# Second pair's scores as single float32 products, under a re-searched table and dearer planner charges

## The chip, the cores and the metric

One core of one Trainium2 chip runs the whole program in one launch. The metric is device time in microseconds. The kernel before took 822.62 us (median of 3 runs, 822.43 to 823.08).

## The reference

The program computes an attention layer and two feed-forward layers on its output, all in float32.

```python
B, H, S, D = 4, 8, 576, 64
scores = scale * q @ k^T                      # per batch and head, 576 x 576
scores = where(block_i >= block_j, scores, -1e9)   # blocks of 64 positions
attn = exp(scores - max) / (sum + 1e-9);  x = attn @ v   # -> 2304 x 512
h = x @ w_in (512 x 2048); g = s * relu(h)**2 + b;  x = g @ w_out
h = max(x @ w1, x @ w2, x @ w3) (512 x 768);  out = h @ w_out2
```

## The kernel before, in words

Attention goes by pairs of heads: 16 pairs (4 batches, 4 pairs each). Columns of the two heads of a pair stand side by side in one tile. For each head there are four score units of 128 queries, 192, 320, 448 and 576 keys wide (`unit`, the last in two products of 288), and one unit for the first 64 queries of both heads (`first`, products of 64 by 64). A unit's maximum is taken by VectorE (`most`), its exponential by ScalarE (`expo`). The exponentials are transposed on TensorE (`turned`, 25 transposes a pair, L628), copied from PSUM, and multiplied with the values (`product`), one pair late.

Scores are made in one of two ways. In pairs 1 to 15 each operand is split into a float32r high part and a low part (`prep_pair`: khi, qhi, klo, q2, qlo), and each unit has two float32r products: one of 128 rows (`K1`, `Q1`) and one of 68 rows (`KQ`, whose last four rows carry the mask). Pair 0 alone is made otherwise (`prep_first`): its loaded rows are float32 operands as they are, 64 rows of data and the mask's rows below, in `xf`, a buffer that is not in use yet, and each unit is one plain float32 product.

The two heads' value products, and the two heads' `first` products, use TensorE as two arrays side by side (64 columns each). Both are gathered in a list and issued together by `side_by_side` wherever the order string has a `|`. This text calls such a run a visit. Value products read 128 rows; `first` reads 64 rows. The results leave PSUM by `put` (into `xf`), from bank 7, which the next pair's first value product needs again.

Behind attention come the feed-forward layers: three passes with plain tiles of 512 tokens (`l1`, `l2`), then tiles of 768 tokens by a seven-product scheme (`seven`) with float32r products of 384 columns (`l2_half`, `l4`). Weights are prepared on the way (`prepare_direct`, `prepare_aside`) and fetched again from a scratch in memory (`next_b`).

Nothing is issued in the order in which it is written. `op` records every operation with its possible engines, a cost on each, its dependencies, and a rank: its number plus the offset of its kind from `CFG['off']`. `Sched.run` then lets each engine take, at each point of the planned time, the ready operation of the lowest rank, and the program is issued in that order; on the chip each engine keeps to it and waits where its operand is late. The order of the steps of a pair is a string: a digit is a score unit, lower-case letters a to e turn exponentials, A to E multiply with values, p prepares the next pair, v loads values, `|` issues the visit. `order0` and `order1` are for pairs 0 and 1, `order` for the others. At the start 60 small products on zeros (`warm`, L1135 makes the zeros) have the highest rank of all: the planner puts one wherever TensorE has nothing else, until the 60 are used up. They are called fillers here. They are instructions in TensorE's queue and take their time, whatever the rest does.

Of the kernel before, what the change touches and what calls it, by code (L numbers as in the profile page):

```python
# [24 lines left out]
C0 = 192  # L25
NU = 4
# [3 lines left out]
EPS = 1e-9  # L30

# [57 lines left out]
def c_pooltt(n):  # L89
    return 2.4 * n + 100  # L90
# [64 lines left out]
class Sched:  # L155
# [45 lines left out]
    def run(self):  # L201
# [26 lines left out]
        while len(order) < n:  # L228
# [54 lines left out]
def tile_attention_moe(ctx: ExitStack, tc: tile.TileContext, qk, vp, w_in, w_out, ms_, b_, w123, w_out2, out):  # L283
# [98 lines left out]
    def load(size, f, eng="SP", after=(), lat=2000, **k):  # L382

        k["after"] = [op(eng, 380, f, lat=lat, after=after, **k)]
        return op("DMA", size / (CFG["rate"] if k.get("kind") in ("w", "w2", "wf") else 330), lambda e: None, lat=1000 + CFG["dm"].get(k.get("kind"), 0), **k)
# [37 lines left out]
    def load_pair(p):  # L423

        b, hp = divmod(p, H // 2)
        R = FIRST[0::2] if p == 0 else [rings["raw"].get() for _ in range(2)]
        if p == 0:

            for i, e_ in enumerate(("SP", "ACT")):
                def f(e, i=i):  # L430
                    (nc.sync if i == 0 else nc.scalar).dma_start(out=R[i].ap[0:64, 0:2 * S], in_=qk[b, hp, 0:64, i])
                load(294912, f, e_, lat=1260, writes=[(R[i], k) for k in ALL])
        else:
            for i in range(2):
                def f(e, i=i):
                    nc.sync.dma_start(out=R[i].ap, in_=qk[b, hp, :, i])
                load(589824, f, lat=2000 if p < 3 else CFG["dlat"], writes=[(R[i], k) for k in ALL])
        return R

    def prep_first():  # L440

        K0, (K, Q, R) = rings["k0"].get(), FIRST
        for x, keys, _, n in parts(0):
            q, q2 = qcols(R.ap, x, 0)[0:64], qcols(Q.ap[:, 0:1024], x, 64)[0:64]
# [3 lines left out]
            op(pick("q2", 0, **hi_cost(n)), 0, f, reads=[(R, k) for k in keys], writes=[(Q, k) for k in keys], kind="prep", lock=True)  # L448
            if x == "a":
                def f(e):  # L450
                    mul_to(e, K0.ap[:, 0:128], K.ap[0:64, 512:640], SCALE)
                op(pick("k0", 0, **hi_cost(128)), 0, f, reads=[(K, k) for k in keys], writes=[(K0, 0)], kind="prep0", lock=True)

                def f(e, q=q):
                    mul_to(e, K0.ap[:, 128:256].rearrange("p (h c) -> p h c", h=2), R.ap[0:64].rearrange("p (h c) -> p h c", h=2)[:, :, 0:64], 1.0)
                op(pick("k0", 0, **hi_cost(128)), 0, f, reads=[(R, k) for k in keys], writes=[(K0, 1)], kind="prep0", lock=True)
        return K0, None, None, None

    def prep_pair(p, R):


        if p == 0:
            return prep_first()
# [49 lines left out]
    def load_values(p):  # L513
# [5 lines left out]
        load(557056, f, lat=2000 if p < 2 else CFG["dlat"], writes=[V])  # L519
        return V  # L520

    def softmax_pair(p, P, DEN):
# [8 lines left out]
        def most(u, m, reads, v, n, axis=AX.X):  # L531
            def f(e):
                nc.vector.tensor_reduce(out=NM.ap[:, u:u + m], in_=v, axis=axis, op=ALU.max, negate=True)  # L533
            op("DVE", c_dve(n), f, reads=reads, writes=[(NM, u + i) for i in range(m)], kind="max")
# [21 lines left out]
        def scores(i, h, views, SB):  # L556
            keys = [(h, x) for x in ("a" if i == 0 else "ab")]
            K, Q, _ = FIRST

            def f(e):  # L560
                for o, c in views:
                    if p == 0:
                        mm(o, Q.ap[:, 512 * h + 128 * i:512 * h + 128 * i + 128], K.ap[:, c], True, True)
# [4 lines left out]
            op("PE", sum(2 * c_mm(c.stop - c.start) if p else c_two(4 * (c.stop - c.start)) for _, c in views), f,  # L568
                    reads=[(t, k) for k in keys for t in (K1, Q1)] + [(Q1, ("l",) + k) for k in keys] + [(KQ, (x,) + k) for k in keys for x in range(2)]
                    if p else [(t, k) for k in keys for t in (K, Q)] + [(K, "m"), (Q, "m")],  # L570
# [38 lines left out]
    def values_pair(p, E, V):  # L609
# [7 lines left out]
        def turn(groups, u):  # L617
# [3 lines left out]
            for g in groups:  # L621
# [11 lines left out]
                op({x: y(n) for x, y in (("ACT", c_act), ("DVE", c_dve)) if x in CFG["pe"]}, 0, f,  # L633
# [12 lines left out]
        def put(O, src, tok):  # L646
            n = src.stop - src.start

            def f(e):
                copy_to(e, xf[:, hp, t0 + tok:t0 + tok + n], O.ap[:, src])  # L650
            after_side.append(lambda: op({x: y(n) for x, y in (("ACT", c_act), ("DVE", c_dve)) if x in CFG["je"]}, 0, f, reads=[O],
                                         writes=[(XF, (hp, b, tok))], after=[i for u in FIRST for i in u.ops] if b > 1 else (), kind="jc"))
# [491 lines left out]
    flat = xf[:].rearrange("p k t -> p (k t)")  # L1144

# [285 lines left out]
    with tc.manual_schedule():  # L1431
# [5 lines left out]
CFG = {'aside': (6, 9, 12, 14, 18, 19, 23),  # L1437
        'aside3': (1, 1, 1, 0, 0, 0, 2, 0, 0, 2, 2, 0, 1, 1, 0, 2),
# [118 lines left out]
```

## Time and profile before

| | |
|---|---|
| median of 3 runs | 822.62 us |
| the profiled execution, its own time | 822.2 us |
| its span, first to last instruction | 820.4 us |
| busy: TensorE, its weight loads, VectorE, ScalarE, GpSimd | 814.6, 741.4, 616.7, 479.3, 64.6 us |
| TensorE's granted clock | full speed |

The profiled execution took 1.8 us more than its span, and 0.4 us less than the median. The span has two large parts: attention up to about 159 us, and the feed-forward layers behind it. In the timeline a row joins like instructions that follow each other: start, time to the modelled end of the last one, engine, line, operation, tiles, form of the first, count. Ends overlap with the next row, so the time that a group takes of TensorE is the start of the next row less its own start. A plain float32 product shows as two records, a float32r product and a transpose as one; the two heads' products of a visit are two instructions with two records each.

### The profile page before, as it was taken

Reading aid. Unit: us, or ns where it says so; the run is one execution under the profiler, and the core shown is the slowest. Engines: PE = TensorE matmul, PEld = TensorE weight load, DVE = VectorE, ACT = ScalarE, POOL = GpSimd, SP = SyncE. Lnnn points to the kernel's source line nnn. Section 1 sums busy time; section 2 is a strip of 40 time slices with the busy share of each in tenths; the row PEclk is TensorE's granted clock in tenths of the full one; section 3 lists DMA queues with packets and bytes.
Section 4 is the critical chain, followed back from the end, with each engine's and each line's share of the span. In section 5 each row is a group of like instructions: output and inputs, shape, how many; then the busy total and the mean of one; then the engine's idle time right before and its main releaser. Section 6 shows DMA issues by size and latency. Waiting matters only on the chain. (4 is left out here: it accounts for less than half of the span.)

```text
span 820.4 us, 14499 instructions
## 1 busy us (share of the span) xinstructions
PE 814.6 (99%) x4898; PEld 741.4 (90%) x4898; DVE 616.7 (75%) x1347; ACT 479.3 (58%) x1100; POOL 64.6 (8%) x57
## 2 busy tenths in 40 slices
PE   9999999999999999999999999999999999999998
PEld 7778887878888899999999999999999899999996
DVE  7889999998778898879967997986557245833551
ACT  6888989986665688689666669622143122412111
POOL 5344254000000000000000000000000000000000
PEclk9999999999999999999999999999999999999999
DMA  7877786465678599899679799899676477666742
GB/s 236 256 253 210 230 275 208 177 192 198 228 262 305 211 302 354 307 353 376 203 271 323 259 319 338 291 306 306 212 232 206 142 228 229 181 194 188 225 128 77
DMA packets 92178, 200.77 MB, mean 245 GB/s; under 512 B 10948, under 2 KB 16452, under 8 KB 92100
## 3 DMA queue, kind: packets, MB, share of 16 engines
q1 hardware_dynamic: 91880, 199.41, 73.2%
q8 instruction: 39, 0.64, 0.3%
q10 hardware_dynamic: 224, 0.43, 0.2%
q14 instruction: 35, 0.29, 0.1%
HBM read 152.24 MB, written 43.85 MB: 239 GB/s over the span
## 5 line engine op out<-in xcount | busy, mean ns | idle before, releaser
L380 PE MATMUL ps<-arena 128*128 128x384 f32 (+4 forms) x3834 | 719.7, 347 | 1.4 <-DVE arena L1135 1.2
L380 PEld LDWEIGHTS ps<-arena 128*128 128x128 f32 x3834 | 668.9, 188 | 43.3 <-issue 1.4
L959 ACT ACTIVATE other<-ps 128x384 f32<-128x384 f32 x154 | 75.0, 487 | 186.8 <-PE ps L380 169.3
L954 DVE TENSOR_TENSOR other<-ps,other 128x384 f32<-128x384 f32 x129 | 71.2, 554 | 106.2 <-PE ps L380 90.0
L377 DVE TENSOR_TENSOR arena<-other,arena 128x384 fp32r<-128x384 f32 (+3 forms) x201 | 117.9, 598 | 5.2 <-ACT arena L364 2.3
L538 ACT ACTIVATE other<-ps,other 128x192 f32<-128x192 f32 (+4 forms) x144 | 77.7, 550 | 14.9 <-DVE other L533 14.5
L366 DVE TENSOR_SCALAR arena<-other 128x384 fp32r<-128x384 f32 (+3 forms) x148 | 60.2, 410 | 29.6 <-PE ps L380 19.7
L372 ACT ACTIVATE other<-ps 128x512 f32<-128x512 f32 (+1 forms) x102 | 55.8, 572 | 40.3 <-PE ps L380 36.2
L533 DVE TENSOR_REDUCE other<-ps 128x1 f32<-128x192 f32 (+4 forms) x144 | 66.9, 513 | 8.1 <-PE ps L380 7.3
L628 PEld LDWEIGHTS ps<-ident,other 128*128 128x128 f32 x400 | 43.9, 141 | 15.4 <-ACT other L538 10.7
L380 PE MATMUL ps<-other 128*64 128x64 f32 (+5 forms) x640 | 55.1, 313 | 0.0
L377 DVE TENSOR_TENSOR other<-other 128x256 fp32r<-128x256 f32 (+1 forms) x125 | 52.7, 433 | 1.6 <-ACT other L364 0.6
L760 ACT ACTIVATE other<-other 128x512 f32<-128x512 f32 x64 | 43.1, 676 | 17.8 <-DVE other L756 17.8
L628 PE MATMUL ps<-ident,other 128*128 128x128 f32 x400 | 53.4, 277 | 0.0
L768 DVE SCALAR_TENSOR_TENSOR other<-other 128x512 uint32<-128x512 uint32 x64 | 43.6, 687 | 6.7 <-ACT other L760 6.2
L364 ACT ACTIVATE other<-other 128x256 fp32r<-128x256 f32 (+2 forms) x95 | 39.0, 426 | 12.2 <-DMA bscr<-other 4.9
L1345 ACT ACTIVATE other<-other,cst 128x384 f32<-128x384 f32 x64 | 44.7, 701 | 0.7
L364 ACT ACTIVATE arena<-other 128x384 fp32r<-128x384 f32 (+1 forms) x66 | 36.4, 562 | 13.2 <-DVE other L377 10.2
L380 PEld LDWEIGHTS ps<-other 128*64 128x64 f32 (+1 forms) x640 | 26.9, 136 | 13.8 <-issue 9.7
L374 DVE COPY other<-ps 128x384 f32<-128x384 f32 (+2 forms) x49 | 28.2, 597 | 14.2 <-ACT other L372 11.9
L377 POOL TENSOR_TENSOR arena<-other,arena 64x1152 fp32r<-64x1152 f32 x11 | 37.8, 3436 | 11.9 <-PE ps L380 7.4
L1330 ACT ACTIVATE other<-other 128x384 f32<-128x384 f32 x48 | 24.8, 520 | 17.3 <-DVE other L954 17.2
(46 smaller groups left out, 426.7 us busy)
## 6 DMA issues: line engine op xcount, KB each, us to landing
arena<-bscr SPq DMA_DIRECT2D x301, 256.0 KB, 3.3
bscr<-other SPq DMA_DIRECT2D x119, 256.0 KB, 4.0
other<-qk SPq DMA_DIRECT2D x30, 576.0 KB, 5.1
other<-w_in SPq DMA_DIRECT2D x24, 512.0 KB, 5.0
other<-w_out SPq DMA_DIRECT2D x22, 512.0 KB, 5.4
other<-w SPq DMA_DIRECT2D x18, 512.0 KB, 6.1
other<-vp SPq DMA_DIRECT2D x16, 544.0 KB, 5.0
other<-pscr SPq DMA_DIRECT2D x24, 192.0 KB, 4.3
```

The source lines that it names most:

```text
L364: nc.scalar.activation(out=dst, in_=src, func=AF.Copy, scale=m)
L366: nc.vector.tensor_scalar(out=dst, in0=src, scalar1=m, scalar2=None, op0=ALU.mult)
L372: nc.scalar.activation(out=dst, in_=src, func=AF.Copy)
L377: eng[e].tensor_tensor(out=dst, in0=a, in1=b, op=ALU.subtract)
L380: nc.tensor.matmul(o, l, r, start=start, stop=stop, **k)
L533: nc.vector.tensor_reduce(out=NM.ap[:, u:u + m], in_=v, axis=axis, op=ALU.max, negate=True)
L538: nc.scalar.activation(out=ev, in_=v, func=AF.Exp, bias=NM.ap[:, u:u + 1], scale=1.0, accum_out=DEN.ap[:, d:d + 1])
L628: nc.tensor.transpose(TB.ap[:, 128 * i:128 * i + 128], x, ident)
L768: nc.vector.scalar_tensor_tensor(out=lo_w, in0=hi_w, scalar=3, in1=lo_w, op0=ALU.logical_shift_left, op1=ALU.bitwise_or)
L954: nc.vector.tensor_tensor(out=out_.ap, in0=bank.ap[:, 0:HN], in1=u.ap, op=ALU.add)
L959: nc.scalar.activation(out=u.ap, in_=bank.ap[:, 0:HN], func=func)
L1345: nc.scalar.activation(out=u.ap, in_=u.ap, func=AF.Identity, scale=s_t, bias=b_t)
```

## The change

Seven things change in the program's text; the rest is the table of numbers.

1. `prep_first` becomes `prep_plain(p, R)`, used for pairs 0 and 1. Pair 1's keys go to `SECOND[0]`, and its queries, scaled, to `SECOND[1]`; both lie in `xf`. Only 64 rows of each are loaded, and the mask's four rows are copied from pair 0's by two small transfers on ScalarE's queue. The splits of pair 1 (khi, qhi, klo, q2, qlo) are gone.
2. `scores` makes one plain float32 product, of 68 rows, for pair 1.
3. Every copy out of `put` from batch 1 on waits until pairs 0 and 1 are done with `xf` (before: from batch 2 on, for pair 0).
4. The planner's charge for entering a visit goes from 92 to 150, for leaving one from 126 to 216 (transposes next) and from 256 to 290.
5. It charges 46 more for each maximum and each copy of transposed tiles (`EV`), and 2.7 instead of 2.4 per column for two-operand work on GpSimd.
6. It plans the loads of queries, keys and values with 400 (240 for the half loads) bytes per ns instead of 330.
7. The table `CFG` is another: order strings, offsets, allowed engines. With `duo: (0,)` the two heads' 192-wide units share one bank and one maximum; `je: ['DVE']` gives every copy of `put` to VectorE (before ScalarE too); hidden high parts (`hhi`) may go to ScalarE too.

```diff
-            c += 92 if not side else 126 if m == "turn" else 256
+            c += 150 if not side else 216 if m == "turn" else 290
...
-        R = FIRST[0::2] if p == 0 else [rings["raw"].get() for _ in range(2)]
-        if p == 0:
+        R = FIRST[0::2] if p == 0 else [SECOND[0], rings["raw"].get()] if p == 1 else [rings["raw"].get() for _ in range(2)]
+        if p < 2:
...
+    def prep_plain(p, R):
+        K0, (K, Q, q_), R = rings["k0"].get(), plain(p), R[1]
+        if p:
+            def f(e):
+                nc.scalar.dma_start(out=K.ap[64:64 + NU], in_=FIRST[0].ap[64:64 + NU])
+            op("ACT", 60, f, reads=[(FIRST[0], "m")], writes=[(K, "m")], lat=2200, kind="mrow")
...
-                    if p == 0:
-                        mm(o, Q.ap[:, 512 * h + 128 * i:512 * h + 128 * i + 128], K.ap[:, c], True, True)
+                    if p < 2:
+                        mm(o, q_[rows, h, 128 * i:128 * i + 128], K.ap[rows, c], True, True)
                         continue
...
-                after=[i for u in FIRST for i in u.ops] if b > 1 else (), kind="jc"))
+                after=[i for u in FIRST + SECOND for i in u.ops] if b else (), kind="jc"))
...
-        'duo': (),
+        'duo': (0,),
-        'je': ['ACT', 'DVE'],
+        'je': ['DVE'],
-        'order': '20DaEbC6|p75AB41||vd|ce3||8',
+        'order': 'C1DaE|bvp7652d4A0cB3e||||||8',
```

TensorE's instructions before and now: 4568 and 4558. The difference is pair 1: 20 products of float32r go (2 of each width 192, 320 and 448 and 4 of width 288, in two parts each), 10 plain ones come. All other counts, 60 fillers among them, stay.

How the start of TensorE's queue read before (fillers are the rows `ps<-arena 128x256`, pair 0's scores the rows from `xf`, `ident` the transposes):

```order
L380 MATMUL ps<-arena 128x256 x24
L380 MATMUL ps<-xf 128x192
L380 MATMUL ps<-arena 128x256 x5
L380 MATMUL ps<-xf 128x320
L380 MATMUL ps<-xf 128x288 x2
L380 MATMUL ps<-xf 128x320
L380 MATMUL ps<-xf 128x448 x2
L380 MATMUL ps<-xf 128x288 x2
L380 MATMUL ps<-xf 128x192
L380 MATMUL ps<-arena 128x256 x19
L628 MATMUL ps<-ident,other 128x128 x8
```

The same place now (pair 1's scores come from `xf` too):

```order
L381 MATMUL ps<-arena 128x256 x32
L381 MATMUL ps<-xf 128x192
L381 MATMUL ps<-xf 128x320
L381 MATMUL ps<-xf 128x288 x2
L381 MATMUL ps<-xf 128x192
L381 MATMUL ps<-xf 128x448
L381 MATMUL ps<-xf 128x288 x2
L381 MATMUL ps<-xf 128x320
L381 MATMUL ps<-xf 128x448
L381 MATMUL ps<-other 64x64 x4
L381 MATMUL ps<-xf 128x320 x2
L381 MATMUL ps<-xf 128x448
```

Eight more fillers stand ahead of the first score, the runs of 5 and of 19 are gone from between pair 0's scores, and pair 1's scores follow at once; the other 28 fillers stand later, as runs of 17, 2, 7 and 2 between the transposes of pairs 0 and 1.

One pair in the steady part of attention on TensorE before, from one visit to the end of the next (`other` with `64x...` is a visit, `arena` are scores; the row `64x64 x2` ahead of `64x128` is `first`, of 64 rows, and `64x64 x10` are value products of 128 rows):

```order
L380 MATMUL ps<-other 64x512 x2
L380 MATMUL ps<-other 64x384 x2
L628 MATMUL ps<-ident,other 128x128 x8
L380 MATMUL ps<-arena 128x320 x2
L380 MATMUL ps<-arena 128x288 x4
L380 MATMUL ps<-arena 128x192 x2
L380 MATMUL ps<-other 64x64 x2
L380 MATMUL ps<-other 64x128 x2
L380 MATMUL ps<-other 64x64 x10
L380 MATMUL ps<-other 64x256 x2
L628 MATMUL ps<-ident,other 128x128 x14
```

And now:

```order
L381 MATMUL ps<-other 64x512 x2
L381 MATMUL ps<-other 64x64 x2
L381 MATMUL ps<-other 64x384 x2
L644 MATMUL ps<-ident,other 128x128 x8
L381 MATMUL ps<-arena 128x320 x2
L381 MATMUL ps<-arena 128x288 x4
L381 MATMUL ps<-arena 128x192 x4
L381 MATMUL ps<-other 64x256 x2
L381 MATMUL ps<-other 64x128 x2
L381 MATMUL ps<-other 64x64 x10
L644 MATMUL ps<-ident,other 128x128 x14
```

`first` went from the head of one visit into the middle of the other, between two value products. Over the whole program visits go from 33 to 32; passages inside a visit from 64 rows to 128 go from 15 to 14, and from 128 rows to 64 from none to 14.

VectorE in one pair of the steady part before (`TENSOR_REDUCE` are maxima, `128x1152` is khi, `SCALAR_TENSOR_TENSOR` qlo, `COPY` of 384 and 512 from PSUM are turned tiles):

```order
L533 TENSOR_REDUCE other<-ps 128x1 x3
L366 TENSOR_SCALAR arena<-other 128x1152
L499 SCALAR_TENSOR_TENSOR arena<-other,arena 64x1024
L533 TENSOR_REDUCE other<-ps 128x1
L374 COPY other<-ps 128x512
L374 COPY other<-ps 128x384
L533 TENSOR_REDUCE other<-ps 128x1 x5
L374 COPY other<-ps 128x384
```

And now (`COPY xf<-ps` is `put`, `TENSOR_TENSOR` is klo, mostly on GpSimd before, `128x2` the joint maximum):

```order
L548 TENSOR_REDUCE other<-ps 128x1 x5
L367 TENSOR_SCALAR other<-other 64x128
L375 COPY other<-ps 128x512
L548 TENSOR_REDUCE other<-ps 128x1 x2
L548 TENSOR_REDUCE other<-ps 128x2
L367 TENSOR_SCALAR arena<-other 128x1152
L375 COPY xf<-ps 128x64
L378 TENSOR_TENSOR arena<-other,arena 64x1152
L375 COPY xf<-ps 128x512
L514 SCALAR_TENSOR_TENSOR arena<-other,arena 64x1024
```

The copies of `put` came to VectorE, the large one behind klo; the copies of 384 columns went to ScalarE (24 before the last maximum, now 2).

## Rows read from the trace of the kernel before

**Rows 1.** The page: busy time, share of the span; granted clock in 40 slices.
```profile
PE 814.6 (99%) x4898; PEld 741.4 (90%) x4898; DVE 616.7 (75%) x1347; ACT 479.3 (58%) x1100; POOL 64.6 (8%) x57
PEclk9999999999999999999999999999999999999999
```
**Rows 2.** Who ended TensorE's idle time: us in total, times, longest.
```profile
PE ps L380 <- DVE arena L1135: 1.2, 1, 1.2
PE ps L380 <- issue: 0.7, 1, 0.7
PE ps L380 <- DVE other L1415: 0.3, 1, 0.3
```
**Rows 3.** The chain that ended last, its longest piece: start, us, what.
```profile
560.66 256.11 PE ps L380 x1365
```
**Rows 4.** Timeline of TensorE at the start.
```profile
1.18 4.44 PE L380 MATMUL ps<-arena 128*128 128x256 f32 x24 [1.18 <-DVE arena L1135]
6.34 0.56 PE L380 MATMUL ps<-xf 128*128 128x192 f32 x2 [0.71 <-issue]
...
7.33 5.07 PE L380 MATMUL ps<-xf 128*128 128x320 f32 x18
12.10 2.56 PE L380 MATMUL ps<-arena 128*128 128x256 f32 x19
14.51 1.26 PE L628 MATMUL ps<-ident,other 128*128 128x128 f32 x8
...
17.77 1.46 PE L380 MATMUL ps<-other 64*64 64x64 f32 x12
```
**Rows 5.** Timeline of TensorE, the last product of pair 0's scores.
```profile
11.91 0.49 PE L380 MATMUL ps<-xf 128*128 128x192 f32 x2
```
**Rows 6.** Timeline of TensorE over one pair of the steady part.
```profile
26.57 1.75 PE L628 MATMUL ps<-ident,other 128*128 128x128 f32 x14
28.07 1.60 PE L380 MATMUL ps<-arena 128*128 128x448 f32 x8
29.52 0.55 PE L628 MATMUL ps<-ident,other 128*128 128x128 f32 x3
29.82 0.74 PE L380 MATMUL ps<-arena 128*128 128x320 f32 x4
30.50 1.73 PE L380 MATMUL ps<-other 128*64 128x512 f32 x8
32.15 1.09 PE L628 MATMUL ps<-ident,other 128*128 128x128 f32 x8
33.00 1.28 PE L380 MATMUL ps<-arena 128*128 128x320 f32 x8
34.21 1.72 PE L380 MATMUL ps<-other 64*64 64x64 f32 x32
35.86 1.75 PE L628 MATMUL ps<-ident,other 128*128 128x128 f32 x14
```
**Rows 7.** Timeline of TensorE, a visit without `first`.
```profile
154.73 1.45 PE L380 MATMUL ps<-other 128*64 128x128 f32 x28
156.11 2.95 PE L628 MATMUL ps<-ident,other 128*128 128x128 f32 x25
```
**Rows 8.** Timeline of TensorE inside a visit, products of 64 columns.
```profile
34.80 0.64 PE L380 MATMUL ps<-other 128*64 128x64 f32 x16
```
**Rows 9.** Timeline of GpSimd and ScalarE at the start: masks, first scaled queries.
```profile
4.42 1.04 POOL L1156 TENSOR_SCALAR_AFFINE_SELECT arena<-arena 128x256 fp32r<-128x256 f32 x2
5.82 0.42 ACT L364 ACTIVATE xf<-xf 64x256 f32<-64x256 f32 x1 [1.18 <-DMA xf<-qk]
6.34 0.83 ACT L364 ACTIVATE xf<-xf 64x768 f32<-64x768 f32 x1
```
**Rows 10.** VectorE's groups by form up to 155 us: busy us, mean ns.
```profile
L377 DVE TENSOR_TENSOR arena<-other,arena 64x1152 fp32r<-64x1152 f32 x3 | 4.0, 1341 | 0.0
L374 DVE COPY xf<-ps 128x512 f32<-128x512 f32 x1 | 0.7, 681 | 0.0
L374 DVE COPY xf<-ps 128x64 f32<-128x64 f32 x1 | 0.2, 215 | 0.0
```

More of the change, by code (lines that the diff above doesn't have):

```diff
@@ L30 @@
 EPS = 1e-9
+EV = 46
 W_REBIAS = 2.0 ** -112
@@ L380, in mm, with load @@
         nc.tensor.matmul(o, l, r, start=start, stop=stop, **k)
-    def load(size, f, eng="SP", after=(), lat=2000, **k):
+    def load(size, f, eng="SP", after=(), lat=2000, rate=330, **k):
         k["after"] = [op(eng, 380, f, lat=lat, after=after, **k)]
-        return op("DMA", size / (CFG["rate"] if k.get("kind") in ("w", "w2", "wf") else 330), lambda e: None, lat=1000 + CFG["dm"].get(k.get("kind"), 0), **k)
+        return op("DMA", size / (CFG["rate"] if k.get("kind") in ("w", "w2", "wf") else rate), lambda e: None, lat=1000 + CFG["dm"].get(k.get("kind"), 0), **k)
     def CFG_E(k, **c):
@@ L436, in f, with plain @@
                     nc.sync.dma_start(out=R[i].ap, in_=qk[b, hp, :, i])
-                load(589824, f, lat=2000 if p < 3 else CFG["dlat"], writes=[(R[i], k) for k in ALL])
+                load(589824, f, rate=400, lat=2000 if p < 3 else CFG["dlat"], writes=[(R[i], k) for k in ALL])
         return R
[L440 to L444, printed above, removed]
+    def plain(p):
+        K, Q = (FIRST, SECOND)[p][0:2]
+        return K, Q, Q.ap if p else Q.ap[:, 0:1024].rearrange("p (h c) -> p h c", h=2)
@@ new lines, in prep_plain, with f @@
+    def prep_plain(p, R):
[4 more added lines that the diff above has]
+            op("ACT", 60, f, reads=[(FIRST[0], "m")], writes=[(K, "m")], lat=2200, kind="mrow")
+            def f(e):
+                nc.scalar.dma_start(out=q_[64:64 + NU], in_=plain(0)[2][64:64 + NU])
+            op("ACT", 60, f, reads=[(FIRST[1], "m")], writes=[(Q, "m")], lat=2200, kind="mrow")
+        for j, (x, keys, _, n) in enumerate(parts(p)):
+            q = qcols(R.ap[:, 0:2 * S], x, 0)[0:64]
+            q2 = (q_[:, :, 0:C0 - 64] if x == "a" else q_[:, :, C0 - 64:] if x == "b" else q_ if x is None else q_[:, x])[0:64]
@@ L533, in f @@
                 nc.vector.tensor_reduce(out=NM.ap[:, u:u + m], in_=v, axis=axis, op=ALU.max, negate=True)
-            op("DVE", c_dve(n), f, reads=reads, writes=[(NM, u + i) for i in range(m)], kind="max")
+            op("DVE", c_dve(n) + EV, f, reads=reads, writes=[(NM, u + i) for i in range(m)], kind="max")
         def expo(u, read, v, n, ev, ekey, d):
@@ L651, in put @@
             after_side.append(lambda: op({x: y(n) for x, y in (("ACT", c_act), ("DVE", c_dve)) if x in CFG["je"]}, 0, f, reads=[O],
[L652 removed]
+                                         writes=[(XF, (hp, b, tok))], after=[i for u in FIRST + SECOND for i in u.ops] if b else (), kind="jc"))
         def tile_of(i, h, k):
```

102 lines of the change are left out of this document (52 added, 50 removed).

## The prediction

> **What bounds the kernel now.** I read the page first. TensorE is busy 814.6 of 820.4 us at full granted clock, VectorE 75%, ScalarE 58% [rows 1]. A busy share can hide waits, so the view of waits came next: TensorE waited 2.2 us in all, 1.9 of them at the very start [rows 2]. The chain that ended last says the same: its last 256 us are one piece of TensorE [rows 3]. So the time is what stands in TensorE's queue, plus the few us at either end, and an edit counts by what it adds to or takes from that queue. What the other engines do counts only where it makes TensorE wait.
>
> The timeline of the start shows where TensorE does nothing useful: zeros until 5.6, a gap of 0.71 before the first score at 6.34, zeros again from 12.10 to 14.51 [rows 4]. Behind that the same pattern repeats: from 26.57 to 35.86 one pair, 9.29 us, each row starting where the one before it leaves off [rows 6]. 14 transposes in 1.50 us (26.57 to 28.07) are 0.107 each, too short for a wait between them. Attention is paced by TensorE too.
>
> **The change part by part.**
>
> **Pair 1's scores.** A plain product's price is in pair 0: from 7.33 to 11.91 run two products of 320 columns, four of 288 and two of 448, together 2688 columns, in 4.58 us [rows 4, 5], or 1.70 ns a column. A pair has twice 192+320+576+448, so 3072 columns: 5.23 us. The two-part form is in rows 6: scores run from 28.07 to 29.52, 29.82 to 30.50 and 33.00 to 34.21, together 1.45 + 0.68 + 1.21 = 3.34 us. The swap adds 1.9 us. Some of the 3.34 is what scores pay because they stand next to transposes and visits, and pair 1's scores will pay some of it too; if that were all of 0.4 us it would be 2.3. I take 2.2, between 1.9 and 2.3. The splits of pair 1 that go free VectorE, ScalarE and GpSimd, and save TensorE nothing by themselves: what they may move comes under the start.
>
> **`first` in the middle of a visit.** Compare two visits. With `first` at its head and then the products of 128, 64 and 256 columns, a visit takes 34.21 to 35.86, 1.65 us for 32 records [rows 6]; the same visit without it takes 154.73 to 156.11, 1.38 us for 28 records [rows 7]. The two small products cost 0.27. Products of 64 columns in a visit follow each other at (0.64 - 0.22) / 7 = 0.06 us, as 16 records are 8 products and 0.22 the length of the last [rows 8]. Two are 0.12, and the remaining 0.15 us is the passage from 64 rows to 128. The trace has no passage from 128 rows back to 64. Its bounds are nothing and, by the nearest row, the same 0.15. I take 0.15, because the passage seen costs this without a wait by any row of the waits. 14 of them add 2.1; one passage fewer the other way takes 0.15. One visit fewer saves what entering and leaving cost, by my estimate about 0.2: the products of the visit of rows 7 have 1408 columns, at 0.06 per 64 some 1.3 us, and it takes 1.38, so 0.1 for leaving, and I put as much on entering. Sum 1.75, between -0.35 (the way back is free) and 1.75.
>
> The Trainium skill's page "TensorEngine Tiling (Array Packing)", section "Tiling Modes" (Key Properties), states that changing the tiling mode drains TensorE, without regard to direction. By that rule the part is 1.75; by what the trace shows of this direction alone it would be -0.35, and no row here tells which. It speaks against this change, and its rival is the first one below.
>
> **The start.** 60 fillers stand in both queues, so they cost the same. What can go is real waiting: 0.71 before the first score. Now eight more fillers stand there; a filler's row is 2.41 us for 19 (12.10 to 14.51), 0.13 each, so eight fill 1.0 us that would be spent waiting anyway [rows 4]. The queries landed at 5.82 [rows 9], and they have to be scaled first: on GpSimd now, which is free of its masks at 4.42 + 1.04 = 5.46, so not later than the data. The rest of pair 0's queries starts on ScalarE at 5.82 instead of 6.34, as two small jobs ahead of it have gone elsewhere. Then pair 1's scores stand ready for TensorE while the first pair goes through maximum, exponential and transposes. The order expects to wait between those transposes all the same, since its fillers of 17, 2, 7 and 2 stand there. I take -0.6, bounds -0.7 (all of that gap) and +1.5 (two gaps of that size where the second pair's exponentials run late; before, this place was covered by the run of 19).
>
> **Steady pairs.** Scores, transposes and value products are the same in number, so nothing is added but the above. VectorE takes over most klo (11 instead of 3) and all copies of `put`, ScalarE the turned copies of 384 columns, GpSimd loses eight klo. I cost this at nothing: TensorE's row has no gap in a pair, and what an engine does behind it is late only if a bank is. The one place where a bank is close is the second rival.
>
> **Feed-forward layers.** The same products in the same number. Splits and loads are placed otherwise, with a shorter planned transfer. Before, waiting here was 0.3 us [rows 2], so there is almost nothing to win and something to lose: 0, bounds -0.5 and +2.5 (eight waits of 0.3).
>
> Sum: 2.2 + 1.75 - 0.6 + 0 = +3.35. On the span of 820.4 that is 823.75; its execution took 1.8 more than its span, 825.55; the median of runs is 0.42 above that execution, so 826.0 us, 0.41% slower.
>
> **Rivals.**
>
> *The way back to 64 rows is free (not slower).* For it: no row shows that direction, and the products on either side are of the same kind, two arrays side by side. Against it: entering, leaving and widening each show a price. Then 2.1 goes and the sum is +1.25: 823.9 us. It decides at 0.03 us a passage, since 1.25 + 14 x 0.03 is 1.65, and 1.65 us is 0.2% of 822.6, about what a measurement of this kernel can tell from no change.
>
> *The large copy of `put` comes late in every pair (slower still).* Bank 7 must be empty before the next visit's first value product. Between visits TensorE has 3.93 us (26.57 to 30.50), and 0.2 less now since 192 columns stand ahead of the visit instead of behind it [rows 6]. In that time VectorE has to get past the copy of 64, klo, and the copy of 512: 0.215 + 1.341 + 0.681 = 2.24 us [rows 10], after what it still has in hand when the visit ends, the joint maximum and khi, another 1 us or so. Margin about half a us. Price: if it is 0.3 late in each of 14 pairs, 4.2 us: 830.2. Queued behind that copy are qlo and the next maxima, and TensorE's scores behind those.
>
> *The start gives much more than the gap (faster).* All 60 fillers are instructions in the queue and cannot be skipped, so a gain of more than the waits of rows 2 has no place. If every wait of rows 2 went and the way back were free, the sum would be 2.2 - 0.35 - 1.9 - 0.3 = -0.35, still no change: 822.3.
>
> **How the numbers follow.** Forecast (826.0, own range 824.6 to 828.0): 0.55. Way back free: 0.20, 823.9. Late copies or other new waits, 830 and above or so: 0.18. Start, or something that I don't see: 0.07. Slower by more than 0.2% (above 824.3) takes the forecast but for a little, and the late copies: 0.72. Within 0.2% takes the free way back and half of the last: 0.23. Faster: 0.05, as no term reaches it. The range goes from 822.9 (a free way back and the start at its best: 2.2 - 0.35 - 0.7 = 1.15, less the 0.5 of the feed-forward layers, 823.3, and a little more) to 830.6 (the late copies, with 0.4 on top).
>
> **What would show it.** In TensorE's timeline of the changed kernel: pair 1's scores as records from `xf`, the ten products in about 5.2 us; a steady pair of 9.29 + 0.15 to 0.3 us; the row of `first` between two value products with a start-to-start time about 0.15 longer on either side than inside the 64s. First score at about 6.4 without a gap before it. Wrong would be the step on `first` if a steady pair takes 9.3 us or less in spite of the passage; the step on the start if the waits of TensorE name ScalarE or VectorE before 26 us; the step on steady pairs if they name VectorE's copies. The whole would be wrong if TensorE's gaps grow in the feed-forward layers.

## The result, and the profile after

The changed kernel takes 828.96 us (median of 4 runs, 828.83 to 829.34), the kernel before on the same chip 822.75 us (4 runs, 822.43 to 823.08): ratio 1.0075, 95% interval 1.0062 to 1.0089. It is slower, as forecast, by 6.2 us where 3.35 were forecast. The spans of the two profiled executions, 827.1 and 820.4 us, differ by 6.7.

The page of the changed kernel, busy time and granted clock, which answers to [rows 1]:

```profile
PE 820.2 (99%) x4898; PEld 744.1 (90%) x4898; DVE 607.6 (73%) x1276; ACT 504.6 (61%) x1145; POOL 38.8 (5%) x59
PEclk9999999999999999999999999999999999999999
```

TensorE is still the bound, at full granted clock throughout. Its waits, against [rows 2], and the pieces of the chain that differ from [rows 3]:

```profile
PE ps L381 <- DVE arena L1151: 1.2, 1, 1.2
PE ps L381 <- ACT xf L365: 0.8, 1, 0.8
PE ps L381 <- ACT other L975: 0.6, 1, 0.6
```

```profile
0.73 5.14 DMA xf<-qk
6.62 1.28 ACT L365
...
193.29 1.90 DVE arena L378 x3
...
566.48 256.46 PE ps L381 x1368
```

Two names are new in the waits: ScalarE's scaled queries (L365) at the start, and its copies of product sums out of PSUM in the seven-product scheme (L975, `out_of`). In the chain the start runs through the load of the queries and then through 1.28 us of ScalarE. The waits in all grew by 0.4 us only (2.2 to 2.6): most of the 6.7 us is not waiting that these rows name, but a longer queue or instructions that follow each other more slowly.

The start of TensorE's timeline, against [rows 4] (the scores of the second pair are the rows `xf` of 68 rows):

```profile
1.18 6.54 PE L381 MATMUL ps<-arena 128*128 128x256 f32 x32 [1.18 <-DVE arena L1151]
7.56 0.49 PE L381 MATMUL ps<-xf 128*128 128x192 f32 x2
8.81 5.11 PE L381 MATMUL ps<-xf 128*128 128x320 f32 x18 [0.76 <-ACT xf L365]
13.85 0.45 PE L381 MATMUL ps<-other 64*64 64x64 f32 x8
14.23 3.07 PE L381 MATMUL ps<-xf 68*128 68x320 f32 x10
17.13 1.26 PE L644 MATMUL ps<-ident,other 128*128 128x128 f32 x10
18.23 0.82 PE L381 MATMUL ps<-xf 68*128 68x192 f32 x4
18.88 0.60 PE L644 MATMUL ps<-ident,other 128*128 128x128 f32 x4
19.32 0.92 PE L381 MATMUL ps<-xf 68*128 68x448 f32 x2
...
22.11 1.14 PE L381 MATMUL ps<-xf 68*128 68x288 f32 x4
23.08 1.04 PE L644 MATMUL ps<-ident,other 128*128 128x128 f32 x8
```

One steady pair, against [rows 6]. It runs from 38.42 to 47.84, 9.42 us. The second visit, 42.10 to 44.17, now has `first` between two value products and takes 2.07; the first one, up to 38.42, is without it and takes 1.38, as the visit of [rows 7]:

```profile
37.04 1.45 PE L381 MATMUL ps<-other 128*64 128x256 f32 x28
38.42 1.75 PE L644 MATMUL ps<-ident,other 128*128 128x128 f32 x14
...
42.10 2.14 PE L381 MATMUL ps<-other 128*64 128x512 f32 x12
44.17 1.09 PE L644 MATMUL ps<-ident,other 128*128 128x128 f32 x8
...
47.84 1.75 PE L644 MATMUL ps<-ident,other 128*128 128x128 f32 x14
```

ScalarE at the start, against [rows 9] (`ACTq` is its queue issuing a transfer). The first row is from the kernel before, where the table is loaded early; the others are from the changed one:

```profile
1.34 1.28 ACT L364 ACT_TABLE_LOAD   x1 [1.34 <-PEq L1550]
...
3.56 1.28 ACTq L455 DMA_DIRECT2D xf<-xf  x1
5.95 0.64 ACTq L451 DMA_DIRECT2D xf<-xf  x1
6.62 1.28 ACT L365 ACT_TABLE_LOAD   x1 [6.62 <-POOL xf L369]
7.91 0.84 ACT L365 ACTIVATE xf<-xf 64x768 f32<-64x768 f32 x1
```

Where the 6.7 us are, cut at like places of both timelines:

| stretch | before | after | difference |
|---|---|---|---|
| to the end of the first like visit | 35.86 | 38.42 | +2.56 |
| 13 pairs from there to the last visit's end | 120.25 | 122.39 | +2.14 |
| last 25 transposes, to the first product of `l1` | 2.71 | 2.82 | +0.11 |
| feed-forward layers, to the end of the span | 661.6 | 663.5 | +1.9 |

(Before: last visit's end 156.11, first `l1` product 158.82. After: 160.81 and 163.63.)

Of the +2.56 of the first stretch, 0.05 is waiting (0.71 before, 0.76 now) and 1.0 is the fillers: the same 60 take 9.34 us before and 10.35 now, each counted from its start to the next start, waits left out. Scores, transposes and visits make the other 1.5. The fillers' pace at the start differs between executions whose queues begin alike: the 24 in front took 4.44 us in the profiled execution of the kernel before [rows 4], and between 5.15 and 5.49 in six kernels of the experiments that have the same 24 in front, as in this one (products of `first` filled up, below):

```profile
1.19 5.32 PE L380 MATMUL ps<-arena 128*128 128x256 f32 x24 [1.19 <-DVE arena L1135]
```

So that 1.0 us may in part come from which executions were profiled, and not from the change.

### The profile page after: what moved, and what is told of

Same layout as the page of the kernel before. It is cut to its first block, busy times and chain, and to the rows that moved or that the text cites. A ratio compares the mean times of both kernels' runs of the same rounds, so it can differ in the third digit from the quotient of the medians.

```text
span 827.1 us, 14455 instructions
## 1 busy us (share of the span) xinstructions
PE 820.2 (99%) x4898; PEld 744.1 (90%) x4898; DVE 607.6 (73%) x1276; ACT 504.6 (61%) x1145; POOL 38.8 (5%) x59
## 4 chain that ended last, share of the span: by engine, by line
PE 93%; DVE 4%; ACT 1%; issue 1%; DMA 1%; POOL 0%; ACTq 0%; DVEq 0%
PE ps L381 87%; PE ps L644 5%; DVE arena L378 1%; DVE other L784 1%; DMA xf<-qk 1%; DVE other L772 0%; DVE other L780 0%; ACT other L776 0%; DVE xf L880 0%; ACT arena L365 0%; DVE arena L367 0%; DVE xf L375 0%; ACT L365 0%; DVE other L548 0%; ACT other L1030 0%
## 5 line engine op out<-in xcount | busy, mean ns | idle before, releaser
L975 ACT ACTIVATE other<-ps 128x384 f32<-128x384 f32 x154 | 74.8, 486 | 138.3 <-PE ps L381 130.8
L970 DVE TENSOR_TENSOR other<-ps,other 128x384 f32<-128x384 f32 x129 | 71.3, 554 | 110.2 <-PE ps L381 93.0
L378 DVE TENSOR_TENSOR arena<-other,arena 128x384 fp32r<-128x384 f32 (+2 forms) x207 | 126.8, 626 | 29.4 <-ACT arena L365 27.6
L365 ACT ACTIVATE arena<-other 128x384 fp32r<-128x384 f32 (+1 forms) x138 | 74.4, 552 | 77.6 <-PE ps L381 59.3
L373 ACT ACTIVATE other<-ps 128x512 f32<-128x512 f32 (+2 forms) x121 | 62.1, 558 | 38.1 <-PE ps L381 29.7
L548 DVE TENSOR_REDUCE other<-ps 128x1 f32<-128x448 f32 (+4 forms) x128 | 65.5, 559 | 6.8 <-PE ps L381 4.5
L378 DVE TENSOR_TENSOR other<-other 128x256 fp32r<-128x256 f32 (+1 forms) x125 | 52.2, 432 | 1.3 <-ACT other L365 0.6
L776 ACT ACTIVATE other<-other 128x512 f32<-128x512 f32 x64 | 42.6, 674 | 12.8 <-DVE other L772 12.6
L367 DVE TENSOR_SCALAR arena<-other 128x384 fp32r<-128x384 f32 (+2 forms) x72 | 32.4, 451 | 12.4 <-PE ps L381 8.5
L365 ACT ACTIVATE other<-other 128x256 fp32r<-128x256 f32 (+2 forms) x78 | 32.9, 439 | 5.0 <-DMA bscr<-other 1.5
L1355 ACT ACTIVATE other<-other 128x384 f32<-128x384 f32 x64 | 32.9, 516 | 0.7
L375 DVE COPY other<-ps 128x512 f32<-128x512 f32 (+2 forms) x30 | 19.3, 650 | 16.4 <-ACT other L373 11.9
L1432 DVE TENSOR_TENSOR other<-other 128x384 f32<-128x384 f32 x54 | 30.0, 556 | 1.5
```

Source lines behind the costliest of these rows:

```text
L365: nc.scalar.activation(out=dst, in_=src, func=AF.Copy, scale=m)
L373: nc.scalar.activation(out=dst, in_=src, func=AF.Copy)
L378: eng[e].tensor_tensor(out=dst, in0=a, in1=b, op=ALU.subtract)
L776: nc.scalar.activation(out=hi_f, in_=hi_f, func=AF.Prelu, scale=W_REBIAS, alpha=W_SIGN)
L970: nc.vector.tensor_tensor(out=out_.ap, in0=bank.ap[:, 0:HN], in1=u.ap, op=ALU.add)
L975: nc.scalar.activation(out=u.ap, in_=bank.ap[:, 0:HN], func=func)
```

## The experiments

All were timed in five rounds against the kernel before on the same chip; ratios are to it, with a 95% interval. The changed kernel itself stands at 828.96.

**`first`, alone and undone.** The kernel before, with `first` put behind the first value product of its visit and nothing else:

```diff
         if side:
+            if len(side) > 1 and side[0][0] == c_two(256):
+                side.insert(1, side.pop(0))
```

> The kernel before, with the two products of `first` issued as the second item of their visit instead of the first; plan, costs and all other orders stay. Theory (every passage between 64 and 128 rows inside a visit costs 0.15 us, either way): a visit with `first` goes from 1.65 to about 1.80 us, a steady pair from 9.29 to 9.44, the whole 15 x 0.15 = +2.2 us, about 825.0. Rival (the way back to 64 rows is free): pair and whole unchanged, about 822.7.

825.20 us, ratio 1.0027 (1.0017 to 1.0038). The visit grew from 1.65 [rows 6] to 1.79, and the pair is 9.44 us (36.95 to 46.39):

```profile
44.60 1.87 PE L380 MATMUL ps<-other 128*64 128x128 f32 x32
46.39 0.88 PE L628 MATMUL ps<-ident,other 128*128 128x128 f32 x6
```

That is the theory's time, and the rival falls: the way from 128 rows back to 64 costs the same as the way out. The other side, the changed kernel with `first` at the head of the visit:

```diff
-            side.append((c_two(256), f, [(K0, 0), (K0, 1)], [SB]))
+            side.insert(0, (c_two(256), f, [(K0, 0), (K0, 1)], [SB]))
```

> The changed kernel, with `first` issued as the head of its visit again; plan, costs and all other orders stay. Theory: one passage fewer in each of 14 visits, a steady pair from 9.43 to 9.28 us, the whole -2.1 us, about 826.9. Rival (the passage is free and the pair's 0.14 comes from waits on the new order of copies): unchanged, about 829.0.

827.21 us, ratio 1.0052 (1.0039 to 1.0065), 1.75 less than the changed kernel (2.1 expected). The visit went from 2.07 to 1.92:

```profile
42.16 1.99 PE L381 MATMUL ps<-other 64*64 64x64 f32 x12
44.08 1.09 PE L644 MATMUL ps<-ident,other 128*128 128x128 f32 x8
```

**No passage at all.** The kernel before, its `first` operands filled up with zeros to 128 rows, so that no product of a visit has 64 rows:

```diff
-    k0=Strip(other, K0AT, 256, lambda t: t[0:64])
+    k0=Strip(other, K0AT, 256)
...
+    for at in K0AT:
+        u = other.take(at, 256)
+        def f(e, u=u):
+            eng[e].memset(u.ap[64:128], 0.0)
```

> The kernel before, with zeros in rows 64 to 127 of the operands of `first`, so that its products read 128 rows like the others of the visit and no passage is left. Theory: 15 passages fewer at 0.15 us, a steady pair from 9.29 to 9.14, the whole -2.2 us, about 820.5; the two more fills at the start cost nothing that shows. Rival (the 0.15 in that visit is not a passage but the small products' own start): unchanged, about 822.7.

821.09 us, ratio 0.998 (0.9972 to 0.9989): faster than both kernels, by 1.7 us against the one before where 2.2 were expected. The visit is 1.50, 0.15 below [rows 6], and this pair 9.14 (26.66 to 35.80):

```profile
34.30 1.57 PE L380 MATMUL ps<-other 128*64 128x64 f32 x32
35.80 1.75 PE L628 MATMUL ps<-ident,other 128*128 128x128 f32 x14
```

Pair by pair against the kernel before, most of this kernel's pairs are 0.12 to 0.15 us shorter; three in a row are not (9.34, 9.39 and 9.21 us, from 81.55 to 109.49, against 9.23, 9.35 and 9.24). There the gain is given back. The changed kernel with the same filling, and with ScalarE's table loaded early (the edit of that is shown under the start):

> The changed kernel with both repairs: `first` on 128 rows by zeros below its operands (no passage in any visit), and ScalarE's table loaded early. Theory: 28 passages at 0.15 us go, -4.2, and -1.2 at the start: 823.5, a steady pair of 9.13 us. Rival (start's end is set elsewhere): 824.7.

825.31 us, ratio 1.0029 (1.0017 to 1.0040), 3.65 less than the changed kernel, where 5.4 were expected. Its visit lost both passages, 2.07 to 1.77 (40.73 to 42.50), and the pair around it takes 9.12 (37.05 to 46.17):

```profile
40.73 1.84 PE L381 MATMUL ps<-other 128*64 128x512 f32 x12
42.50 1.09 PE L644 MATMUL ps<-ident,other 128*128 128x128 f32 x8
```

Both passages together are worth 0.30 us by this, and here the visit is entered in the same way with and without them. (With `first` moved to the head or away from it, what the visit is entered with changes too, so the split of the 0.30 into two times 0.15 rests on the entry costing the same either way.) The first like visit ends 1.37 us earlier than in the changed kernel, in an execution in which the 32 fillers took 5.56 us and TensorE still waited 0.66 for ScalarE at the start. The 13 pairs behind it take 120.06 us instead of 122.39, 2.3 less where 13 times 0.30 is 3.9: the longest are 9.81 and 9.56 (92.17 to 111.54), where the changed kernel has 9.54 and 9.43.

Of 120 us from 30 to 150, VectorE is busy 116.4 in this kernel, 115.2 in the changed one and 112.4 before, so a shorter TensorE queue may run into VectorE there. That is argued and not shown: no row names VectorE, and from 80 to 156, where the longest of these pairs lie, it is busy 74.2 to 74.4 of 76 us in all three.

**The start.** The two transfers of the mask's rows on SP's queue instead of ScalarE's:

```diff
-                nc.scalar.dma_start(out=K.ap[64:64 + NU], ...)
+                nc.sync.dma_start(out=K.ap[64:64 + NU], ...)
...
```

> The changed kernel, with the two transfers of mask rows issued on SyncE's queue instead of ScalarE's; plan unchanged. Theory (ScalarE's queue stands at the second of them until the queries land at 5.9 us, and only then loads its table, so the second part of pair 0's queries is scaled at 7.9 instead of 5.9): table load before 5 us, that scaling at about 5.9, the first product of 320 columns at 7.6 or earlier instead of 8.81, the whole -0.9 to -1.5 us, about 827.8. Rival (the pairs' chain of maxima and exponentials sets the end of the start, not that scaling): the first 320 comes earlier, but the steady part begins where it did and the whole is unchanged, 829.0.

838.03 us, ratio 1.0179 (1.0165 to 1.0193), 9 us slower than the changed kernel where about 1 less was expected. The start of it goes as the theory has it: with ScalarE's queue free the table loads at 1.35, the rest of pair 0's queries is scaled at 6.20, and the first score starts at 6.74 with pair 0 in one run. But SP's queue issued the masks only at 6.64 and 10.34, behind other loads, and TensorE waited 6 us for them (the first row is SP's queue):

```profile
10.34 0.68 SPq L451 DMA_DIRECT2D xf<-xf  x1
...
6.74 5.47 PE L381 MATMUL ps<-xf 128*128 128x192 f32 x20 [0.16 <-POOL xf L369]
12.14 0.45 PE L381 MATMUL ps<-other 64*64 64x64 f32 x8
18.63 5.88 PE L381 MATMUL ps<-xf 68*128 68x320 f32 x10 [6.04 <-DMA xf<-xf]
24.31 1.91 PE L644 MATMUL ps<-ident,other 128*128 128x128 f32 x8
```

The ten records take 5.7 us (18.63 to 24.31), in the changed kernel 2.9. The view of stretches says why (columns: busy time of TensorE, its loads, VectorE, ScalarE, GpSimd, then the granted clock, the DMA share and GB/s):

```profile
14.00:16.00 2.00, 0.00 (x0) 0.00 (x0) 0.00 (x0) 0.67 (x5) 2.00 (x3) 0.61 1.19 342
...
26.00:28.00 2.00, 2.00 (x10) 1.91 (x9) 0.00 (x0) 0.92 (x2) 0.00 (x0) 0.50 0.41 123
28.00:30.00 2.00, 2.00 (x14) 1.63 (x13) 1.18 (x2) 1.47 (x4) 0.00 (x0) 0.98 0.00 0
```

TensorE stood still from about 12.6, the granted clock fell to 0.50, the lower of its two levels, and was back only at 28. From 18.63 on that is 9.4 us at half speed, 4.7 lost; with 6.0 of waiting and 1.7 won before (pair 0 done at 12.14 instead of 13.85) that makes +9.0, and 838.03 less 828.96 is 9.07.

The gentle way leaves the transfers and makes ScalarE load its table ahead of them, by a small operation of its own:

```diff
+    nc.vector.memset(cst[:, 2:4], 0.0)
+    nc.scalar.activation(out=cst[:, 2:3], in_=cst[:, 3:4], func=AF.Copy)
```

> The changed kernel, with one small copy on ScalarE ahead of the two transfers of mask rows, so that its table is loaded at about 1.4 us instead of 6.6; nothing else moves. Theory (the start lost its gain to ScalarE's queue, where the table load of 1.28 us stood behind a transfer that waits for the queries): pair 0's second scaling at 6.6 instead of 7.9, first product of 320 columns at about 7.6 instead of 8.81, the whole -1.2 us, about 827.7. Rival (the chain of maxima and exponentials of the first pairs sets the end of the start): product of 320 earlier, the steady part where it was, 828.9.

827.92 us, ratio 1.0062 (1.0049 to 1.0074), 1.0 less than the changed kernel, near the theory's 1.2; the rival falls, as the first like visit ends at 37.52 instead of 38.42. The table loads at 1.39, the queries are scaled at 6.80 instead of 7.91, and the wait for ScalarE at the start is gone. What the first score stands behind now is the fillers:

```profile
1.19 6.68 PE L381 MATMUL ps<-arena 128*128 128x256 f32 x32 [1.19 <-DVE arena L1151]
7.70 5.33 PE L381 MATMUL ps<-xf 128*128 128x192 f32 x20
```

**The plain pair alone.** The kernel before with parts 1 to 3 of the change (pair 1's scores plain, its mask rows by transfers), old table and old charges:

```diff
-        if p == 0:
+        if p < 2:
...
-                    if p == 0:
+                    if p < 2:
...
-                after=[i for u in FIRST for i in u.ops] if b > 1 else (), kind="jc"))
+                after=[i for u in FIRST + SECOND for i in u.ops] if b else (), kind="jc"))
```

> Pair 1's scores as plain products alone, with the table and the planner's charges of the kernel before; 60 fillers, `first` at the head of its visit. Theory (sum of the queue): +2.3 us for the products, and up to +1.5 for the late table load on ScalarE, no change in the visits and the feed-forward layers: 825.0 to 826.5. Rival (the plain products stand where TensorE waited, so they cost nothing): 822.8 or less.

833.95 us, ratio 1.0143 (1.0127 to 1.0158): 11 us slower, outside what the theory and the rival expected. Feed-forward layers take what they took before; all of it is in attention. Its waits:

```profile
PE ps L644 <- ACT other L553: 3.3, 3, 1.7
PE ps L381 <- issue: 2.2, 1, 2.2
...
PE ps L644 <- ACT other L373: 0.7, 2, 0.6
```

In the old table ScalarE alone scales pair 0's queries, now behind the masks' transfers and the table load; the first score starts at 8.69, and behind that transposes wait for its exponentials. After the wait of 2.16 the granted clock was at its lower level here too, from the end of the stretch from 8 to 10 (0.91) on:

```profile
10.00:12.00 2.00, 2.00 (x5) 1.32 (x5) 0.49 (x1) 1.07 (x4) 0.00 (x0) 0.50 1.02 307
12.00:14.00 2.00, 2.00 (x7) 1.37 (x6) 0.97 (x2) 0.43 (x3) 1.05 (x1) 0.73 1.04 419
```

The sum of what is named: 2.2 for the plain products, 1.45 more at the first score (2.16 less 0.71 [rows 4]), 4.0 for ScalarE's rows, some 1.7 for the granted clock (what 0.91, 0.50 and 0.73 leave of three stretches of 2 us): 9.4 of 11.3 us between the spans. To see how much hangs on ScalarE's queue, the same kernel with the early table (the diff above):

> The kernel before with the plain float32 scores of pair 1 alone (table and charges as before), and ScalarE's table now loaded by a small operation of its own ahead of the transfers; TensorE's order is that of the same kernel without this. Theory (its 11 us over the kernel before start with the table load that stands behind the mask transfers on ScalarE's queue, 5.3 us later than before): the 2.2 us gap before the first score shrinks to below 1, ScalarE scales at about 6.9 instead of 8.0, and what hangs on it behind goes with it: 833.95 - 2 to - 4, so 830 to 832. Rival (the loss is in how the old order strings make transposes wait for pair 1's exponentials, whatever the start does): the gap shrinks but the waits behind it grow by as much, 833 to 834.5.

832.59 us, ratio 1.0118 (1.0098 to 1.0138), single runs from 830.27 to 833.92. Neither side wins cleanly. The start went as the theory has it: the gap 0.99, pair 0 done 3.0 us earlier. The waits behind it stayed as they were, 1.71 and 1.12 in place of 1.72 and 1.12, so the start is not what makes them; that the old order strings are is what remains, and was not tested by itself. And after the first of them the granted clock fell in this execution, which it had not done in the one above:

```profile
29.03 2.04 PE L644 MATMUL ps<-ident,other 128*128 128x128 f32 x11 [1.71 <-ACT other L553]
```

```profile
30.00:32.00 2.00, 2.00 (x8) 1.20 (x6) 0.69 (x1) 1.43 (x4) 0.00 (x0) 0.50 0.82 336
...
36.00:38.00 2.00, 2.00 (x16) 2.00 (x15) 1.11 (x2) 1.11 (x3) 0.00 (x0) 0.87 0.76 263
```

That is some 3.4 us at what the granted clock leaves of these stretches, and took the 3.0 back. The run of 830.27 is the one of the four whose mean granted clock is 1.00.

**Table and charges apart.** Old charges, GpSimd price and rates in the changed kernel (parts 4 to 6 undone):

```diff
-                    c += 150 if not side else 216 if m == "turn" else 290
+                    c += 92 if not side else 126 if m == "turn" else 256
...
```

> The changed kernel with the planner's old charges, GpSimd price and transfer rates (parts 4 to 6 of the change undone); table and plain pair stay. Theory (charges only reorder what stands ready; table and charges were chosen together, so apart they cost): the start is drawn up otherwise (24 fillers ahead of the first score, as before), visits keep `first` in the middle as the order string says so; 829 to 832. Rival (the new charges are themselves what costs): below 828.

835.68 us, ratio 1.0163 (1.0143 to 1.0183): slower than the theory and the rival expected. First score at 8.95 after a gap of 2.27, and a transpose that waits 2.15 for ScalarE at 45.54. TensorE's waits add up to 8.6 us here and to 2.6 in the changed kernel; the spans differ by 5.7. The other way round, the new charges and price in the kernel before (parts 4 and 5):

```diff
-                    c += 92 if not side else 126 if m == "turn" else 256
+                    c += 150 if not side else 216 if m == "turn" else 290
...
```

> The kernel before with the new charges for visits, maxima, copies and GpSimd (parts 4 and 5 of the change alone); table, two-part scores of pair 1 and transfer rates as before. Theory (with a table that was chosen for the old charges, new ones move instructions by chance): 823 to 826, `first` still at the head of its visit, no loss by passages. Rival (dearer waiting instructions give a better order by themselves): below 822.

831.93 us, ratio 1.0113 (1.0099 to 1.0126): slower than expected too, with `first` still at the head of its visits, which still take 1.65. From 82 us on the pairs take 9.5 to 11.8 us, before 9.2 to 9.4. Waits for ScalarE's exponentials, 3.1 us in 5 places up to 152 us, are named there; that is a third of the 9.8 us between the spans, and no row names the rest. So neither undoing the charges in the changed kernel nor putting them alone into the one before is a gain: each costs more than the whole change. The table alone, with old charges and two-part scores, was not run.

**The feed-forward layers.** The changed kernel with hidden high parts (`hhi`, the high parts of the feed-forward layers' inner values) on VectorE alone, as before:

```diff
-               'hhi': ['ACT', 'DVE'],
+               'hhi': ['DVE'],
```

> The changed kernel with the hidden layer's high parts on VectorE alone, as before (the planner makes a new order for the feed-forward layers; attention's queue stays). Theory (what the feed-forward layers lost, 1.9 us from the first l1 product to the end, is waits of TensorE on VectorE and ScalarE at a few handovers, from the shared placement): the wait of 0.58 us at 566 us goes and the whole is -1 us, about 828. Rival (it comes from the other parts of the table, or from the run): within 0.5 us of 829.0.

832.41 us, ratio 1.0116 (1.0102 to 1.0130). The theory falls: with the order that the planner makes without it, the kernel is 3.5 us slower, so the sharing is not what was lost. Waits for ScalarE's copies out of PSUM (L975) grew to 2.1 us, and one of 1.35 for VectorE's additions out of PSUM (L970, `add_to`) came at 574.52. Neither line is a hidden high part: those are made from SBUF by the helper of L365 and L367. So the wait at 566 us, which the expectations name after hidden parts, is for such a copy. Then all the numbers of the table that place work in these layers, taken from the kernel before (first and last of them):

```diff
-CFG = {'aside': (8, 11, 14, 15, 17, 18, 23),
+CFG = {'aside': (6, 9, 12, 14, 18, 19, 23),
...
-        'xs': 14}
+        'xs': 8}
```

> The changed kernel, with those numbers of its table that place the feed-forward layers' work (where weights are prepared and fetched, the offsets of l1, l2, u, w, xn and the like, hhi on VectorE alone) taken from the kernel before; start, strings of the order, engines of attention and charges stay as changed. Theory (the 1.9 us that the changed kernel loses behind attention come from those numbers): 829.0 - 1.9, so 827.1, range 826.4 to 827.8; the distance from the first product of l1 to the last matmul back to what it is in the kernel before, the wait for ScalarE's hidden parts near 566 us gone. Rival (the loss comes from the state in which attention leaves the engines, which this does not touch): 828.4 to 829.5.

828.92 us, ratio 1.0076 (1.0062 to 1.0090): the theory falls again, and the time is the same to 0.1 us. But it is not lost in the same places. The wait at 566 us is gone and the end is nearly as short as before; instead there is this, where the kernel before has no wait:

```profile
312.13 1.31 PE L381 MATMUL ps<-arena 128*128 128x384 f32 x6 [0.58 <-ACT other L975]
314.35 1.84 PE L381 MATMUL ps<-arena 128*128 128x384 f32 x9 [0.91 <-ACT other L975]
```

Matmul by matmul against the kernel before, this place costs it 1.9 us. The kernel before with new charges loses 1.6 us at the same place, though its numbers for these layers are the old ones. The kernels that keep the old table and charges (`first` moved, or filled, or the plain pair alone) lose nothing in these layers: 661.6 to 661.8 us against 661.6. So in these runs the old numbers cost nothing behind the attention that they were drawn up with, and something behind the two others.

## Why the prediction was right, and where not

*The whole.* The direction is right, and for the reason given: the scores and `first`, 3.95 of the forecast, are there. The size is not: 828.96 lies above the forecast's own range (824.6 to 828.0), by a start that gained nothing and by the feed-forward layers. It lies inside the whole range only because that reaches to 830.6 for late copies of `put`, which did not come; that much is luck.

*What bounds the kernel.* Right for attention: what `first` and the scores cost is what they put into TensorE's queue. It says less of the experiments with another plan, where pairs grew by more than the waits name.

*Pair 1's scores, +2.2.* Right. The ten products take 2.90 (14.23 to 17.13), 0.65 (18.23 to 18.88), 0.75 (448 columns: 2.79 from 19.32 to 22.11 less 17 fillers of 0.12) and 0.97 (22.11 to 23.08): 5.27 us, where 5.23 were worked out. Against the 3.34 of the two-part form that is +1.9, the lower bound; no row shows the further 0.3.

*`first`, +1.75.* Right, and with it the rival of a free way back falls. Both directions cost 0.15 us: 1.65 to 1.79 when one way back is added, 2.07 to 1.92 when one is taken out, 1.65 to 1.50 when the way out goes, 2.07 to 1.77 when both go. The 13 steady pairs grew by 2.14 in all. What one visit and one passage fewer save, 0.35 in the sum, was not measured by itself. The Trainium skill's rule that a change of tiling mode drains TensorE ("TensorEngine Tiling (Array Packing)", section "Tiling Modes") agrees with these rows. That rule of the Trainium skill names neither a direction nor a price; both are from the rows.

*The start, -0.6.* Wrong, in sign too. Taking 2.2 for the scores from the +2.56 of the first stretch, and the share of `first` outside the steady pairs (1.75 - 2.14 = -0.4), leaves about +0.8; with 1.9 for the scores it is 1.1. The step that failed: "The rest of pair 0's queries starts on ScalarE at 5.82 instead of 6.34, as two small jobs ahead of it have gone elsewhere." It counted the jobs that left ScalarE's queue and not the two transfers that came to it, which the description of the change names. The second of them is issued at 5.95, when the load of the queries (5.14 us from 0.73) has landed, and the table load of 1.28, before at 1.34 and beside the loads, stands behind it at 6.62. So the queries are scaled at 7.91. The Trainium skill's page "ScalarE: Activation LUTs", section "What ACT_TABLE_LOAD costs", has 1283 ns for that load, as the row here. (The row names GpSimd as what ended the wait of 6.62. With the transfers gone from this queue, the scaling starts at 6.20, before GpSimd's own at 6.25, so it was the queue.) So the wait of 0.71 went, and one of 0.76 came.

Loading the table early takes that wait away and gives back 1.0 us, and yet no -0.6 comes of it, because a second step was mis-sized: "0.13 each, so eight fill 1.0 us that would be spent waiting anyway". At 0.13 eight already fill more than the gap of 0.71, and the price is that of a later row: the 24 in front take 4.44 us in [rows 4], 0.185 each, and the 32 take 6.4 until the first score (1.18 to 7.56), 0.20 each. In the changed kernel ScalarE is later still (8.75), so they hide; with the table early the first score stands behind them until 7.70, where about 6.4 was forecast. The sign that was named, a wait for ScalarE before 26 us, did come.

*Steady pairs, 0, and the late copy of `put`.* Right: no wait names it. VectorE's copy of 512 ends 1.44 us before the visit at 42.10 needs its bank, three times the margin that was estimated:

```profile
39.99 0.67 DVE L375 COPY xf<-ps 128x512 f32<-128x512 f32 x1
```

*Feed-forward layers, 0.* Mis-sized: +1.9, inside the bounds of -0.5 to +2.5, which were drawn for eight waits of 0.3. By its own sign the whole would be wrong if TensorE's gaps grew here; they went from 0.3 to 0.6 us, one wait for another, which is 0.3 of the 1.9. Matmul by matmul it is 0.86 up to 206 us, where the chain runs through VectorE (`DVE arena L378`), 0.0 from there to 553, 0.5 at the wait of 566, and 0.54 behind the last matmul. "The same products in the same number" was true and did not bear on it. Two experiments exclude simple causes: undoing neither the hidden parts on ScalarE nor all the new numbers for these layers gives the 1.9 back. Every kernel with the changed table or the changed charges loses about 1.6 us or more here, and none with the old table and charges does, so by these runs it goes with the order of attention ahead of these layers; which of the moved instructions is the late one stays open.

*What was not asked at all:* how much of the change the new table pays back. The plain pair costs 11 us under the old table and the whole change 6.2, so parts 4 to 7, charges, rates and table, together give back some 5. The 2.2 for plain products was near for TensorE's queue, and far too little for the kernel with the old table.

## What to carry to other kernels

Count a moved transfer in the queue that issues it, and look at what stands behind it there: a table load that used to lie beside the first loads became part of the chain. A run of products of one row count is worth 0.15 us per change of it in this kernel; filling the odd ones up with zeros was the only edit here that beat both kernels. An order that was searched for one program may not outlive an edit that makes the planner draw it up anew: each part of this change that was run alone was slower than the whole.

## What the runs showed of the hardware

A passage between 64 and 128 rows inside a visit costs 0.15 us in either direction; the rows before the change had only the way from 64 to 128. The granted clock fell to its lower level (0.50, 1.2 GHz) after TensorE had waited 6.0, 2.2 and 1.7 us and stayed there for about 3 to 13 us; yet the same wait of 1.7 us, in the same instruction order, left it at 1.00 in another execution, and so did waits of 2.27 and 2.15 us in the changed kernel with old charges. By these rows a wait of about 2 us was followed by a further loss of some 1.7 and 3.4 us, an estimate from the granted clock, or by none. And 32 fillers at the start took 6.5, 6.7 and 5.4 us in three kernels with the same 32 in front (changed, early table, masks on SP), though the row of the granted clock reads 1.00 there. In the first two they follow each other at 0.21 us until 6.7 and 7.1 us, in the third until 4.1, and at 0.12 behind that; why is open.
